# The remainder of the weights of tiles 2 to 15 computed on GpSimd, in a kernel whose list of instructions is made by a planner

## The chip, the core and the metric

The kernel runs on one core of a Trainium2 chip. The core has four engines that compute: TensorE (PE in the profile; its weight loads are PEld), VectorE (DVE), ScalarE (ACT) and GpSimd (POOL). SyncE (SP) starts the DMA transfers. Each engine works through its own queue in order, and the engines wait for each other by semaphores. The metric is the device time of one execution in microseconds; several runs are made, and their median counts.

## What is computed

Two stages follow one another: a linear recurrence over the sequence for each head, and a two-layer network on its output.

```python
for t in range(S):                                   # S = 768
    cur = einsum('bhd,bhe->bhde', u * k[t], v[t])
    y[t] = einsum('bhd,bhde->bhe', r[t], state + cur)
    state = w[..., None] * state + einsum('bhd,bhe->bhde', k[t], v[t])
x = y as (3072 tokens, 384)                          # 4 sequences, 8 heads of 48
h = x @ w_in                                         # 384 -> 2048
g = maximum(h, 0) + alpha * minimum(h, 0)
out = g @ w_out                                      # 2048 -> 384
```

All inputs and the output are 32-bit floats.

## The kernel before

**Tiles and stages.** The sequence is cut into 6 chunks of 128 tokens (`C`, `L`). For a chunk, the recurrence becomes a few matrix products for each of 4 pairs of heads (`attention(c, q, at)`), with the state carried from chunk to chunk. The network then works on the 512 tokens of a chunk (4 sequences of 128), in 16 tiles of 128 hidden units. A *step* is one tile of one chunk: `m_in(n)` makes the hidden units (three products for each of 3 blocks of rows, line 571) and applies the slope (lines 577 to 582); `m_out(n)` multiplies by the second matrix and adds up in `acc` (line 602), two to three steps later.

**Rounded part and rest.** A product of full precision is made of three products of a faster format: each operand is split into its rounded part and the rest. `xh` and `xl` are those of the activations, `gh` and `gl` those of the hidden units, `wh` and `wl` those of the weights. `wl` is the weight minus `wh`.

**The weights.** They come as words of eight bytes (64-bit floats), 768 KB for a tile. `weights(i, need)` turns tile i into 32-bit floats and splits it, once for all chunks: ScalarE makes a scaled magnitude (line 307), VectorE shifts it (309) and puts in the low bits and the sign (311, 314), ScalarE rounds to `wh` (317), VectorE subtracts to `wl` (318). The two halves of a tile's results stay in the memory on the core; the loaded words (`wraw`) and the 32-bit form (`wx`) have two buffers each. A `wx` buffer is free for the tile after next once line 318 has read it, a `wraw` buffer once line 314 has.

**Steps in order.** Chunks 0 and 1 take turns: tiles 0 to 8 of chunk 0, tiles 0 to 8 of chunk 1, tiles 9 to 15 of chunk 0, tiles 9 to 15 of chunk 1. So tile i of the first nine is needed at step i, and tiles 9 to 15 at steps 18 to 24. Then come chunks 2 to 5, 16 steps each.

**The planner.** The kernel doesn't issue instructions as it describes them. `add(engine, us, function, reads, writes, rank)` records a piece with an assumed duration. `Plan.in_order` runs a list schedule forward over all pieces (each engine takes the most urgent piece that is ready), then backward to get new urgencies, 12 times, keeps the round with the earliest end and sorts the pieces by their planned start. That list is the program: each engine's order is fixed by it, and the chip follows it however long things really take. Assumed durations on VectorE and ScalarE are shortened by a small overlap (0.08 and 0.1 us) when the engine is set free; GpSimd's are not. The planner holds nothing of one engine slowing another.

**Fillers.** Where the planner sees TensorE idle before the first piece of the network, it puts in small matmuls on the identity (`warm`, line 662 in the profile), which compute nothing that is used.

**GpSimd's own work.** Some tables at the start (lines 229 to 258 and 641); and for chunks 2 to 5 two products for each pair of heads (lines 394 and 396), which VectorE sums (line 400) into `cu`. ScalarE spreads `cu` over `base` (427), VectorE puts the scores over it (435), and TensorE uses `base` (479). For chunk 2, the piece of line 394 also names `wh` of tile 12 as something that it reads, so that in the list it stands behind it; on the chip it doesn't read it.

Of the kernel before, what the change touches and what calls it, by code (L numbers as in the profile page):

```python
# [56 lines left out]
class Plan:  # L57
# [12 lines left out]
    def add(self, eng, us, fn, r=(), w=(), rank=0.0, kb=0.0):  # L70
        p = Piece(eng, us, fn, r, w, rank, kb)
        for ref, wr in p.uses:
            b, part = ref if isinstance(ref, tuple) else (ref, None)
            log = self.log.setdefault(b, [])
            for other, opart, owr in log:
                if other is not p and (wr or owr) and (part is None or opart is None or part == opart):
                    p.after.add(other)
            log.append((p, part, wr))
        self.pieces.append(p)
        return p  # L80
# [92 lines left out]
def rwkv_prelu_kernel(ctx: ExitStack, tc, rk, vkr, wP, uP, u, wall, alpha, w, r_all, k_all, v_all, oT):  # L173
    nc = tc.nc
# [10 lines left out]
    add = plan.add  # L185

    def sb(shape, name, bufs, dt=F32):
        return plan.buf(lambda: wk.tile(shape, dt, name=name, bufs=bufs), name, bufs)
# [98 lines left out]
    def raw_weights(i, rank, behind=()):  # L287
        t = raws[i] = sb([128, 2 * DM, 2], "wraw", 2, U32)
        load(t, lambda: nc.sync.dma_start(t().rearrange("p f a -> p (f a)"), wall[i].bitcast(U32)), 768, rank, behind)
        return t  # L290

    def weights(i, need):


        raw = raws.get(i) or raw_weights(i, need - 9)
        h, l, t = wh[i], wl[i], sb([128, 2 * DM], "wx", 2, U32)

        def bits():
            return t()

        def x():
            return t().bitcast(F32)

        def hx():
            return h().rearrange("p k f -> p (k f)")

        add("ACT", 0.92, lambda: nc.scalar.activation(x(), raw()[:, :, 1].bitcast(F32), AF.Abs, scale=2.0 ** -112),
            r=[raw], w=[t], rank=need - 3 - 60 * (i == 0))
        add("DVE", 0.56, lambda: nc.vector.tensor_scalar(bits(), bits(), 3, None, op0=ALU.logical_shift_left), w=[t],
            rank=need - 2 - 60 * (i == 0))  # L310
        add("DVE", 0.95, lambda: nc.vector.scalar_tensor_tensor(
            out=bits(), in0=raw()[:, :, 0], scalar=29, in1=bits(), op0=ALU.logical_shift_right, op1=ALU.bitwise_or),
            r=[raw], w=[t], rank=need - 2 - 60 * (i == 0))
        add("DVE", 0.95, lambda: nc.vector.scalar_tensor_tensor(
            out=bits(), in0=raw()[:, :, 1], scalar=0x80000000, in1=bits(), op0=ALU.bitwise_and, op1=ALU.bitwise_or),
            r=[raw], w=[t], rank=need - 2 - 60 * (i == 0))
        add("ACT", 0.85, lambda: nc.scalar.activation(hx(), x(), AF.Copy), r=[t], w=[h], rank=need - 3 - 60 * (i == 0))
        add("DVE", 0.95, lambda: nc.vector.tensor_tensor(
            out=l().rearrange("p k f -> p (k f)"), in0=x(), in1=hx(), op=ALU.subtract), r=[t, h], w=[l], rank=need - 2 - 60 * (i == 0))


# [356 lines left out]
    for i in range(NF):  # L678
        jobs.append((need[i] - 8, 1, lambda i=i: weights(i, need[i])))
# [160 lines left out]
```

## Time and profile before

| | |
|---|---|
| median of 3 runs | 517.65 us (517.52 to 518.13) |
| the profiled run | 516.91 us |
| its span in the trace | 515.2 us |
| VectorE's line 318 | 16 instructions, 15.3 us in sum |
| GpSimd's lines 394 and 396 | 16 instructions each, 20.4 and 19.2 us in sum |

The span runs from the first to the last instruction that the profiler records; the time of the run is a little longer. A row such as `43.13 0.95 DVE L318 TENSOR_TENSOR wl<-wx,wh 128x768 ...` in the view in order of time says: at 43.13 us, for 0.95 us, VectorE ran the instruction of line 318, which wrote `wl` and read `wx` and `wh`; what stands in brackets behind it is how long the engine had been idle and who ended that. Small instructions on VectorE overlap a little, so that the start of the next one is the better measure of what one costs. In the view by source, three numbers with strokes are the shortest, median and longest duration in ns, followed by the first and the last start.

### The profile page before, as it was taken

To read this page: it belongs to the slowest core of one execution; us is meant where nothing else is said; L and a number is where in the kernel's file an instruction comes from. 1 tells how busy PE (TensorE), PEld (TensorE's weight loads), DVE (VectorE), ACT (ScalarE), POOL (GpSimd) and SP (SyncE) were. 2 spreads that over 40 slices of the span, in tenths; PEclk is the share of its full clock that TensorE was granted. 3 is DMA by queue.
4 is the path that set the end of the run, shared out by engine and by line. 5 is a ranking of instruction groups with operands and counts; after the bars stand their busy time and mean duration, and the time that the engine had idled before them with its cause. 6 is when DMAs were issued, how large, how long until landed. Compare 5 with 4: busy or idle time off the path is not lost.

```text
span 515.2 us, 9052 instructions
## 1 busy us (share of the span) xinstructions
PE 504.3 (98%) x3544; PEld 400.8 (78%) x3544; DVE 328.2 (64%) x577; ACT 242.8 (47%) x525; POOL 46.9 (9%) x54
## 2 busy tenths in 40 slices
PE   8999999999999999999999999999999999999994
PEld 6777887888877877787787777787777778888883
DVE  5899999999567885955674655674554453333331
ACT  2757665767455452543352652542643332322222
POOL 3020022010011020120110112030000000000000
PEclk9799999999999999999999999999999999999998
DMA  8864676551323721422120322120220000100001
GB/s 235 259 214 158 218 235 195 185 168 46 117 69 90 224 87 45 143 68 86 53 65 19 125 67 84 49 82 0 70 76 4 0 2 1 61 1 1 0 1 66
DMA packets 24880, 47.26 MB, mean 92 GB/s; under 512 B 4096, under 2 KB 12416, under 8 KB 24832
## 3 DMA queue, kind: packets, MB, share of 16 engines
q1 hardware_dynamic: 24832, 46.62, 28.7%
q8 instruction: 30, 0.49, 0.4%
q14 instruction: 18, 0.15, 0.1%
HBM read 37.96 MB, written 6.29 MB: 86 GB/s over the span
## 4 chain that ended last, share of the span: by engine, by line
PE 93%; DVE 3%; ACT 1%; DMA 1%; issue 1%; SPq 0%; DVEq 0%; ACTq 0%
PE acc L602 39%; PE hp L571 39%; PE A L411 3%; PE y L479 2%; PE y L474 2%; PE A L479 1%; PE A L420 1%; PE y L463 1%; PE y L488 1%; PE y L468 1%; ACT base L427 1%; DMA wp<-wP 1%; PE acc L384 1%; DVE raw L369 1%; PE acc L662 1%
## 5 line engine op out<-in xcount | busy, mean ns | idle before, releaser
L578 DVE SCALAR_TENSOR_TENSOR g<-hp,alph,g 128x512 f32<-128x512 f32 x96 | 71.9, 749 | 113.3 <-ACT g L577 113.1
L577 ACT ACTIVATE g<-hp 128x512 f32<-128x512 f32 x96 | 57.3, 597 | 145.8 <-PE hp L571 145.5
L571 PE MATMUL hp<-xh,wh 128*128 128x512 f32 x288 | 115.7, 402 | 0.8 <-DMA xh<-xh 0.8
L571 PE MATMUL hp<-xl,wh 128*128 128x512 f32 x288 | 113.8, 395 | 0.0
L571 PE MATMUL hp<-xh,wl 128*128 128x512 f32 x288 | 113.7, 395 | 0.0
L582 DVE TENSOR_TENSOR gl<-g,gh 128x512 fp32r<-128x512 f32 x96 | 68.6, 714 | 41.5 <-ACT gh L581 41.3
L581 ACT ACTIVATE gh<-g 128x512 fp32r<-128x512 f32 x96 | 60.6, 631 | 70.8 <-DVE g L578 70.5
L602 PE MATMUL acc<-gh,wh 128*128 128x512 f32 x288 | 85.2, 402 | 0.2 <-ACT gh L581 0.2
L602 PE MATMUL acc<-gh,wl 128*128 128x512 f32 x288 | 83.3, 396 | 0.0
L602 PE MATMUL acc<-gl,wh 128*128 128x512 f32 x288 | 82.7, 394 | 0.0
L571 PEld LDWEIGHTS hp<-xh,wh 128*128 128x128 f32 x288 | 54.0, 188 | 14.4 <-DMA xl<-xl 0.9
L602 PEld LDWEIGHTS acc<-gl,wh 128*128 128x128 f32 x288 | 54.0, 188 | 12.8
L602 PEld LDWEIGHTS acc<-gh,wl 128*128 128x128 f32 x288 | 53.8, 188 | 13.0
L571 PEld LDWEIGHTS hp<-xl,wh 128*128 128x128 f32 x288 | 54.1, 188 | 12.7
L571 PEld LDWEIGHTS hp<-xh,wl 128*128 128x128 f32 x288 | 54.1, 188 | 12.0
L602 PEld LDWEIGHTS acc<-gh,wh 128*128 128x128 f32 x288 | 52.4, 188 | 13.3 <-ACT gh L581 0.7
L427 ACT ACTIVATE base<-ident,cu 128x128 f32<-128x128 f32 x192 | 59.9, 390 | 1.0 <-DVE cu L400 0.7
L394 POOL TENSOR_TENSOR rr<-rr,kk 128x384 f32<-128x384 f32 x16 | 20.4, 1273 | 275.0 <-DMA kk<-vkr 136.5
L369 DVE TENSOR_TENSOR raw<-raw,W 112x512 f32<-112x512 f32 x45 | 36.7, 832 | 0.0
L435 DVE COPY_PREDICATED base<-strict,A 64x128 f32<-64x128 uint8 (+1 forms) x96 | 26.9, 343 | 0.8
L524 DVE TENSOR_TENSOR xl<-y,xh 48x256 fp32r<-48x256 f32 (+1 forms) x38 | 17.5, 462 | 3.0 <-ACT xh L523 2.6
L396 POOL TENSOR_TENSOR rr<-rr,utab 128x384 f32<-128x384 f32 x16 | 19.2, 1202 | 1.3
(102 smaller groups left out, 436.0 us busy)
## 6 DMA issues: line engine op xcount, KB each, us to landing
wraw<-wall SPq DMA_DIRECT2D x16, 768.0 KB, 4.9
raw<-rk SPq DMA_DIRECT2D x45, 224.0 KB, 2.9
v<-vkr SPq DMA_DIRECT2D x24, 192.0 KB, 3.6
kk<-vkr SPq DMA_DIRECT2D x24, 192.0 KB, 3.2
rr<-vkr SPq DMA_DIRECT2D x16, 192.0 KB, 2.5
oT<-o SPq DMA_DIRECT2D x12, 256.0 KB, 2.2
oT<-g SPq DMA_DIRECT2D x6, 256.0 KB, 2.7
xh<-xh SPq DMA_DIRECT2D x36, 32.0 KB, 2.2
```

Of the source, the lines that this page charges most:

```text
L369: add("DVE", 0.72, lambda t=t, tab=tab: nc.vector.tensor_tensor(out=t(), in0=t(), in1=tab().broadcast_to([112, B, L]), op=ALU.mult), r=[W[ ...
L394: add("POOL", 1.2, lambda: nc.gpsimd.tensor_tensor(out=rt(), in0=rt(), in1=k(), op=ALU.mult), r=[k] + ([wh[12]] if c == 2 else []), w=[rt] ...
L396: add("POOL", 1.2, lambda: nc.gpsimd.tensor_tensor(out=rt().rearrange("p (g b) e -> p g b e", g=2), in0=rt().rearrange("p (g b) e -> p g b ...
L427: add("ACT", 0.39, lambda g=g, b=b: nc.scalar.activation(base[g]()[:, b].rearrange("p (a t) -> p a t", a=2), ident().rearrange("p (a t) -> ...
L435: add("DVE", 0.42 if at_part is parts[0] else 0.28, lambda g=g, x=at_part: nc.vector.copy_predicated(base[g]()[x], strict4()[x], A[g]()[x] ...
L524: add("DVE", us + 0.1, lambda: nc.vector.tensor_tensor(out=view(l), in0=psum(), in1=view(h), op=ALU.subtract), r=[src] + refs(h), w=refs(l ...
L571: nc.tensor.matmul(hp(), a[i]()[:, k], x[c]()[:, k], start=(k == 0 and j == 0), stop=(k == NK - 1 and j == 2))
L577: add("ACT", 0.6, lambda: nc.scalar.activation(g(), hp(), AF.Copy), r=[hp], w=[g], rank=n - 100)
L578: add("DVE", 0.75, lambda: nc.vector.scalar_tensor_tensor(out=g(), in0=hp(), scalar=alph()[:, i:i + 1], in1=g(), op0=ALU.mult, op1=ALU.max ...
L581: add("ACT", 0.64, lambda: nc.scalar.activation(gh(), g(), AF.Copy), r=[g], w=[gh], rank=n - 100)
L582: add("DVE", 0.73, lambda: nc.vector.tensor_tensor(out=gl(), in0=g(), in1=gh(), op=ALU.subtract), r=[g, gh], w=[gl], rank=n - 99)
L602: nc.tensor.matmul(banks[k](), a[i]()[:, NK + k], x(), start=(begin and j == 0), stop=(end and j == 2))
```

## The change

```diff
@@ -315,7 +315,9 @@
         add("ACT", 0.85, lambda: nc.scalar.activation(hx(), x(), AF.Copy), r=[t], w=[h], rank=need - 3 - 60 * (i == 0))
-        add("DVE", 0.95, lambda: nc.vector.tensor_tensor(
+
+        on, eng, us = ("DVE", nc.vector, 0.95) if i < 2 else ("POOL", nc.gpsimd, 2.3)
+        add(on, us, lambda: eng.tensor_tensor(
             out=l().rearrange("p k f -> p (k f)"), in0=x(), in1=hx(), op=ALU.subtract), r=[t, h], w=[l], rank=need - 2 - 60 * (i == 0))
```

The subtraction at line 318 is recorded for GpSimd, with 2.3 us in place of 0.95, for tiles 2 to 15; tiles 0 and 1 keep VectorE. What it computes is the same. The planner then makes the whole list anew with the other engine and duration, so that the order of other pieces, and the fillers, can come out different too.

## The prediction

> **What bounds the kernel now.** I read the page first: the span, the busy shares and the shares of the chain that ended last. Then I cut the span into five stretches with the view of busy time by windows, whose columns are PE, PEld, DVE, ACT and POOL busy time (with instruction counts), the granted clock, the DMA share and GB/s.
>
> ```profile
> span 515.2 us, 9052 instructions
> PE 504.3 (98%) x3544; PEld 400.8 (78%) x3544; DVE 328.2 (64%) x577; ACT 242.8 (47%) x525; POOL 46.9 (9%) x54
> ...
> PE 93%; DVE 3%; ACT 1%; DMA 1%; issue 1%; SPq 0%; DVEq 0%; ACTq 0%
> ```
>
> ```profile
> 0.00:31.00 31.00, 27.78 (x247) 22.58 (x247) 22.48 (x46) 16.80 (x48) 5.69 (x22) 0.89 0.76 222
> 31.00:45.00 14.00, 12.91 (x121) 9.50 (x121) 13.92 (x22) 9.34 (x20) 1.64 (x1) 1.00 0.81 267
> 45.00:130.00 85.00, 85.00 (x582) 68.21 (x581) 83.67 (x130) 56.93 (x112) 7.89 (x6) 1.00 0.51 165
> 130.00:508.60 378.60, 378.59 (x2600) 300.48 (x2598) 208.16 (x383) 159.18 (x346) 31.67 (x26) 1.00 0.19 58
> 508.60:515.20 6.60, 0.00 (x0) 0.00 (x0) 0.00 (x0) 0.60 (x1) 0.00 (x0) 0.71 0.35 124
> ```
>
> The reader is to see two things in the windows. From 45.0 to 508.6 us TensorE has 0.01 us without work (85.00 of 85.00, then 378.59 of 378.60): its matmuls, not VectorE, set this length. And VectorE is full (83.67 of 85.00) just in 45 to 130, while TensorE is full beside it: a busy VectorE that TensorE does not wait for. What VectorE can give back lies only where TensorE still has gaps, in 31 to 45: 14.00 - 12.91 = 1.09 us. So the span is 31.0 + 14.0 + 463.6 + 6.6 = 515.2 us. The profiled run took 516.91 us, so 1.71 us lie around the span; the median of the three runs, 517.65, is 0.74 above that run.
>
> **What goes from VectorE.** The subtraction at line 318 is one group. Its row in the view by source (min/median/max ns, first and last start):
>
> ```profile
> L318 DVE TENSOR_TENSOR wl<-wx,wh x16: 946/952/1098, 27.2 to 128.7; 128x768 fp32r<-128x768 f32 x16
> ```
>
> Two of the 16 stay. Instructions overlap on VectorE: in the rows below L318 starts at 43.13 and the next one at 43.99, so one costs 0.86 us of the engine. 14 x 0.86 = 12.0 us leave VectorE, nearly all between 43 and 130 us, where TensorE has no gap. Worth to the span there: 0. No DMA goes with the step, and none is issued by it.
>
> ```profile
> 42.47 0.74 DVE L578 SCALAR_TENSOR_TENSOR g<-hp,alph,g 128x512 f32<-128x512 f32 x1
> 43.13 0.95 DVE L318 TENSOR_TENSOR wl<-wx,wh 128x768 fp32r<-128x768 f32 x1
> 43.99 1.02 DVE L499 TENSOR_TENSOR kk<-kk,wtok 128x384 f32<-128x384 f32 x2
> ...
> 41.98 0.84 ACT L317 ACTIVATE wh<-wx 128x768 fp32r<-128x768 f32 x1 [0.20 <-DVE wx L314]
> ...
> 43.93 0.96 PE L602 MATMUL acc<-gh,wh 128*128 128x512 f32 x3 [0.25 <-ACT gh L581]
> 44.96 0.39 PE L571 MATMUL hp<-xh,wl 128*128 128x512 f32 x1
> ```
>
> In 31 to 45 one single instance goes, tile 2's, at 43.13. The last gap of TensorE before 45 (0.25 us, ended at 43.93 by `gh`) hangs on the L578 at 42.47, which stands ahead of it. So the 0.86 us come too late to close a gap: 0 gained in this order.
>
> **What is added to GpSimd.** No row shows a 128x768 subtraction there. The nearest are its 128x384 products, half the size, and a tiny one:
>
> ```profile
> L394 POOL TENSOR_TENSOR rr<-rr,kk x16: 1010/1021/2445, 70.4 to 346.1; 128x384 f32<-128x384 f32 x16
> L396 POOL TENSOR_TENSOR rr<-rr,utab x16: 1002/1274/1519, 72.1 to 347.1; 128x384 f32<-128x384 f32 x16
> L258 POOL TENSOR_TENSOR uw<-up,wp x2: 284/431/578, 7.1 to 7.5; 48x4 f32<-48x4 f32 x2
> ```
>
> Lower end: 0.43 us of fixed cost (L258) plus 764/380 of (1.01 - 0.43) gives 1.6 us. Upper end: twice the 1.65 us that L394 took in the full stretch (rows below), 3.3 us. Twice the undisturbed 1.02 is 2.04, and I take 2.1, nearest to the medians. 14 x 2.1 = 29 us of GpSimd time from 43 us on; it worked 7.89 of 85 us there, so there is room.
>
> For tile 2: `wh` is done at 41.98 + 0.84 = 42.82, the result then at 44.9 (1.6: 44.4; 3.3: 46.1), and its first reader ran at 44.96. Between nothing and 1.2 us of a TensorE stall, once; the list knows a duration of 2.3, and TensorE has matmuls of tiles 0 and 1 left to put in front. I take 0.2. Nothing gets below zero by this term, as a later `wl` speeds nothing up.
>
> For tile 8, the last with little time in hand, the rows are:
>
> ```profile
> 86.49 0.96 DVE L318 TENSOR_TENSOR wl<-wx,wh 128x768 fp32r<-128x768 f32 x1
> ...
> 88.99 0.39 PE L571 MATMUL hp<-xh,wl 128*128 128x512 f32 x1
> ```
>
> 1.5 us between result and reader. GpSimd's extra 1.1 us fits; 3.3 us would be 0.8 late. Tiles 9 to 15 are read from step 18 on, which the chain in order of time has at 128.00, with 4.2 us from step to step:
>
> ```profile
> 96.52 1.82 DVE L318 TENSOR_TENSOR wl<-wx,wh 128x768 fp32r<-128x768 f32 x2
> ...
> 128.00 2.09 PE hp L571 x9
> ...
> 132.19 2.09 PE hp L571 x9
> ```
>
> Tile 9 is made at 97.5 and read at 128; tile 15, the last, is made at 129.7 and read six steps later, at 153: covered by more than 20 us.
>
> **The added wait.** L318 on GpSimd waits for ScalarE's L317. Behind it stand L394 and L396 of the third chunk, and VectorE's L400 waits for these. Before, GpSimd ran the first two pairs at 70 and 77 us, far ahead of L400; in the list L394 of that chunk stands behind `wh` of tile 12, so now subtractions are in front of it. Cover:
>
> ```profile
> 111.37 0.55 DVE L400 TENSOR_REDUCE cu<-rr 128x8 f32<-128x384 f32 x1
> 111.83 0.68 DVE L582 TENSOR_TENSOR gl<-g,gh 128x512 fp32r<-128x512 f32 x1
> ...
> 118.77 0.85 PE L602 MATMUL acc<-gl,wh 128*128 128x512 f32 x3
> 145.27 0.31 PE L479 MATMUL y<-base,v 128*48 128x128 f32 x1
> ```
>
> TensorE reads what comes of `cu` at 145.27, 33 us later, and the `gl` queued behind L400 at 118.77, 6.3 us after it is done. A late pair of 2 to 3 us costs nothing; without that cover it would cost its 2 to 3 us.
>
> **What GpSimd does to VectorE.** This is the term that the list does not hold. The three pairs in the full stretch, with VectorE beside them:
>
> ```profile
> 70.40 1.65 POOL L394 TENSOR_TENSOR rr<-rr,kk 128x384 f32<-128x384 f32 x1 [37.76 <-DMA kk<-vkr]
> ...
> 77.56 1.65 POOL L394 TENSOR_TENSOR rr<-rr,kk 128x384 f32<-128x384 f32 x1 [4.42 <-DMA kk<-vkr]
> ...
> 114.40 1.02 POOL L394 TENSOR_TENSOR rr<-rr,kk 128x384 f32<-128x384 f32 x1 [33.78 <-DMA rr<-vkr]
> 115.50 1.22 POOL L396 TENSOR_TENSOR rr<-rr,utab 128x384 f32<-128x384 f32 x1
> ...
> 78.88 0.87 DVE L369 TENSOR_TENSOR raw<-raw,W 112x512 f32<-112x512 f32 x1
> 80.34 1.10 DVE L318 TENSOR_TENSOR wl<-wx,wh 128x768 fp32r<-128x768 f32 x1
> 114.81 1.03 DVE L309 TENSOR_SCALAR wx<-wx 128x768 uint32<-128x768 uint32 x1
> 116.10 1.43 DVE L311 SCALAR_TENSOR_TENSOR wx<-wraw,wx 128x768 uint32<-128x768 uint32 x1
> ```
>
> ```profile
> L309 DVE TENSOR_SCALAR wx<-wx x16: 537/552/1026, 21.2 to 122.7; 128x768 uint32<-128x768 uint32 x16
> L311 DVE SCALAR_TENSOR_TENSOR wx<-wraw,wx x16: 943/950/1430, 22.9 to 125.2; 128x768 uint32<-128x768 uint32 x16
> L369 DVE TENSOR_TENSOR raw<-raw,W x45: 669/684/1502, 7.3 to 386.5; 112x512 f32<-112x512 f32 x45
> ```
>
> Against the medians the second pair cost VectorE 0.19 + 0.15 = 0.34 us and the third 0.48 + 0.48 = 0.96; beside the first nothing on VectorE was long. A pair moves as much data as one subtraction, so I take the mean, 0.43 us for each tile, with 0 and 0.96 as what pairs showed, and 2.04 (VectorE held for two whole products) as the far end. Net for VectorE: -0.86 + 0.43, with ends -0.86 and +1.18 us a tile. By the middle value the six tiles 3 to 8 leave VectorE 2.6 us ahead by 88 us, and it waits for TensorE: 0.
>
> The Trainium skill, page "SBUF — State Buffer", section "Who interferes with whom", says that GpSimd and VectorE share a port pair as an exclusive lock, and that the one that comes second is fully blocked. The 1.43 against 0.95 us at 116.10 agree in kind; that every GpSimd instruction blocks VectorE for its length the three pairs do not show, and what it would make of the sum is the first rival.
>
> **Sum.** 0 (to 31) + 0.2 (31 to 45) + 0 (45 to 508.6, fed TensorE) + 0 (the end: no instruction of it changes) = 515.4 us of span, 517.1 us for the run, and 517.65 + 0.2 = 517.85, given as **517.9 us**, as a median. About 0.2%, 1.0 us, is what a measurement of this kernel can tell from no change.
>
> **The rivals.**
>
> *VectorE blocked for nearly the whole subtraction* (slower). If VectorE loses c us per tile, it falls behind the old order by c - 0.86 a tile. Six tiles and 1.5 us in hand at tile 8: it costs 6 x (c - 0.86) - 1.5, from c = 1.11 us on. At c = 1.6, halfway from there to 2.04, that is 2.9 us: 520.6; at 2.04 it is 5.6 us, 523.3. For it: one instruction of 2 us leaves VectorE no turn in its middle, as a pair does, and most VectorE work of the weights (L309, L311) is of the kind that was held. Against it: c was 0.96 at most in three pairs. Chance 0.24.
>
> *A late `wl`* (slower or unseen). If a subtraction takes 3.3 us against the 2.3 in the list, TensorE waits 1.0 us at the first tile whose reader stands right behind; later tiles share this wait, since TensorE is then late already: 518.9. For: both early L394 took 1.65. Against: ScalarE had tile 2's `wh` done 0.31 us before VectorE took it up, and GpSimd is free sooner. Chance 0.10, half of it beyond 1.0 us.
>
> *A shorter start* (faster). The list is made anew, with 0.86 us less on VectorE before 45. If it puts tile 2's other steps and what follows forward, the 1.09 us of gaps go, and part of the filler matmuls of the start with them:
>
> ```profile
> 27.16 2.67 PE L662 MATMUL acc<-ident 128*128 128x256 bf16 x23
> 34.37 0.47 PE L571 MATMUL hp<-xh,wh 128*128 128x512 f32 x1 [0.76 <-DMA xh<-xh]
> ```
>
> 1.09 + 0.5 of the 2.67 gives 516.1. For: VectorE is full (13.92 of 14.00). Against: the larger gap, 0.76 us, ended with a DMA, and the fillers lie before any step that changes. Chance 0.24.
>
> **How the numbers follow.** The forecast, within 1.0 us of before, gets 0.42, with its own range 516.7 to 518.6; the rivals 0.24, 0.10 and 0.24. Faster by over 0.2%: 0.24, the shorter start. Slower: 0.24 and half of 0.10, 0.29. Within: 0.42 and the other half, 0.47. The range reaches to the shorter start's 516.1 and a little below, and to the blocked VectorE's 520.6: 515.7 to 520.6; outside lie a still shorter start (0.08) and c beyond 1.6 (0.10).
>
> **What would show it.** L318 should stand 14 times on POOL at 1.6 to 3.3 us, twice on DVE; TensorE's busy time in 45 to the end should be its length, and 31 to 45 hold about 1 us of gaps. VectorE's L309, L311 and L369 should be longer in sum by 14 x 0.43 = 6 us; 14 us or more would make the first rival, with TensorE's gaps between 50 and 90 us ended by VectorE's `xl`, `wx` or `raw`. Gaps ended by POOL `wl` L318 would make the second; a filler group shorter than 23 and no gap in 31 to 45 the third. The forecast is wrong if TensorE shows more than 1 us of new gaps behind 45, or works less before it.

## The result and the profile after

The changed kernel takes 529.44 us (median of 4 runs, 528.24 to 530.86) against 517.59 us before: a ratio of 1.0231, 95% interval 1.0205 to 1.0257, or 11.8 us more. The forecast was 517.9, with a range up to 520.6.

First the page of the changed kernel: its span, the busy shares, and the shares of the chain.

```profile
span 528.7 us, 9029 instructions
PE 509.4 (96%) x3536; PEld 402.9 (76%) x3536; DVE 333.8 (63%) x563; ACT 241.4 (46%) x525; POOL 71.5 (14%) x68
...
PE 81%; DVE 12%; issue 3%; DMA 1%; ACT 1%; SPq 0%; DVEq 0%; ACTq 0%
```

14 subtractions have left VectorE, some 12 us, and it is busy 5.6 us longer than before (333.8 against 328.2). Its share of the chain went from 3% to 12%. TensorE stands still for 528.7 - 509.4 = 19.3 us in place of 10.9, and works 5.1 us longer for the same products and fewer fillers; one reason is that half of its clock was granted for 10.2 us at the start and for 3.4 us at 131 us, in the kernel before for 6.8 us at the start alone (the end left out). Where it stands still, the busy time by windows tells (columns as in the prediction):

```profile
31.00:45.00 14.00, 11.79 (x118) 8.50 (x114) 13.92 (x22) 8.08 (x14) 1.67 (x2) 1.00 0.65 211
45.00:90.00 45.00, 41.79 (x328) 32.17 (x327) 43.20 (x55) 27.06 (x62) 14.70 (x7) 1.00 0.58 193
90.00:130.00 40.00, 36.80 (x220) 28.59 (x218) 36.26 (x42) 22.23 (x39) 16.07 (x10) 1.00 0.43 146
130.00:200.00 70.00, 69.82 (x521) 55.40 (x523) 48.59 (x90) 34.34 (x80) 11.51 (x9) 0.98 0.32 102
200.00:300.00 100.00, 100.00 (x776) 79.24 (x771) 64.81 (x123) 44.12 (x103) 11.48 (x10) 1.00 0.24 71
```

The gaps are in 31 to 130 us: 2.21 + 3.21 + 3.20 = 8.6 us, where there was 1.1. From 200 us on TensorE is full as before. The 6.4 us behind 45 us lie where GpSimd does the subtractions. The gaps before 45 us stand ahead of its first one (at 44.15 us) and have another cause (experiment 3).

The subtraction itself, in the view by source, and rows of VectorE that grew, in the groups by line and shape (busy us in sum, mean ns of one; the means before were 832, 979, 560 and 581):

```profile
L320 POOL TENSOR_TENSOR wl<-wx,wh x14: 1817/1846/3932, 44.1 to 139.1; 128x768 fp32r<-128x768 f32 x14
L320 DVE TENSOR_TENSOR wl<-wx,wh x2: 953/956/959, 27.7 to 37.6; 128x768 fp32r<-128x768 f32 x2
```

```profile
L371 DVE TENSOR_TENSOR raw<-raw,W 112x512 f32<-112x512 f32 x45 | 38.9, 887 | 1.6 <-DMA raw<-rk 1.5
L311 DVE SCALAR_TENSOR_TENSOR wx<-wraw,wx 128x768 uint32<-128x768 uint32 x16 | 24.2, 1510 | 0.2
...
L501 DVE TENSOR_TENSOR kk<-kk,wtok 128x384 f32<-128x384 f32 x20 | 13.5, 680 | 0.0
...
L309 DVE TENSOR_SCALAR wx<-wx 128x768 uint32<-128x768 uint32 x16 | 12.0, 748 | 2.7 <-ACT wx L307 2.7
```

(Lines from 318 on have moved by two: the subtraction is now line 320, and lines 307 to 317 are as they were.) One subtraction takes 1.85 us on GpSimd in the median: not the trouble. Line 311, one of the steps that stayed, has a mean of 1510 ns, where it had 979. Why shows in the order of time, GpSimd's and VectorE's rows at two places:

```profile
81.74 1.83 POOL L320 TENSOR_TENSOR wl<-wx,wh 128x768 fp32r<-128x768 f32 x1 [6.87 <-ACT wh L317]
...
96.71 1.83 POOL L320 TENSOR_TENSOR wl<-wx,wh 128x768 fp32r<-128x768 f32 x1 [7.93 <-ACT wh L317]
...
82.09 2.30 DVE L311 SCALAR_TENSOR_TENSOR wx<-wraw,wx 128x768 uint32<-128x768 uint32 x1
...
96.86 2.50 DVE L311 SCALAR_TENSOR_TENSOR wx<-wraw,wx 128x768 uint32<-128x768 uint32 x1
```

GpSimd began at 96.71 and ended at 98.54. VectorE's L311 began at 96.86 and ended at 99.36, that is 0.82 us, about its own length, after GpSimd's end: it made next to no progress until the subtraction was over. So did the one at 82.09. Each subtraction starts when ScalarE has `wh`. Beside 11 of the 14, one VectorE instruction was held like this: in seven cases the next tile's 309 (one operand) or 311 (two operands), in the others `kk`, `raw` or `gl`, all of which read from the memory on the core. These 11 took 14.4 us longer than the usual length of their kind. Three subtractions held nobody. The Trainium skill, "SBUF — State Buffer", section "Who interferes with whom", states that VectorE and GpSimd share a port pair as an exclusive lock. That the one that comes second is fully blocked it says of VectorE's two-port modes; here line 311, which reads two operands, shows the same.

It goes the other way too. GpSimd's first subtraction came while VectorE was busy, whose instructions kept their usual lengths, and took twice its usual time:

```profile
44.15 3.93 POOL L320 TENSOR_TENSOR wl<-wx,wh 128x768 fp32r<-128x768 f32 x1 [12.33 <-ACT wh L317]
...
43.70 1.02 DVE L501 TENSOR_TENSOR kk<-kk,wtok 128x384 f32<-128x384 f32 x2
44.64 0.68 DVE L371 TENSOR_TENSOR raw<-raw,W 112x512 f32<-112x512 f32 x1
45.24 0.68 DVE L584 TENSOR_TENSOR gl<-g,gh 128x512 fp32r<-128x512 f32 x1
```

Last, who held TensorE up, in the view of waits (in total, times, longest), and two windows around the longest:

```profile
PE hp L573 <- DVE g L580: 3.4, 2, 2.6
PE acc L386 <- DVE g L379: 1.7, 2, 0.9
PE acc L664 <- POOL ident L233: 1.5, 1, 1.5
PE y L490 <- DVE kk L501: 1.4, 1, 1.4
PE y L465 <- DVE base L440: 0.9, 2, 0.8
PE hp L573 <- POOL wl L320: 0.8, 1, 0.8
```

```profile
125.00:130.00 5.00, 2.58 (x11) 1.58 (x9) 5.00 (x6) 2.76 (x7) 1.74 (x2) 1.00 0.11 38
130.00:135.00 5.00, 4.82 (x14) 3.85 (x15) 4.88 (x11) 3.50 (x10) 3.27 (x2) 0.66 0.15 39
```

TensorE waited for a late `wl` once, 0.8 us (tile 2's, the slow one above). The longest wait is for line 580: the slope of the hidden units, which reads an `hp` bank and so frees it. It has nothing to do with weights; it stands behind them in VectorE's queue:

```profile
126.27 1.19 POOL L396 TENSOR_TENSOR rr<-rr,kk 128x384 f32<-128x384 f32 x1 [0.72 <-DMA rr<-vkr]
...
126.49 1.77 DVE L311 SCALAR_TENSOR_TENSOR wx<-wraw,wx 128x768 uint32<-128x768 uint32 x1
128.19 0.43 DVE L437 COPY_PREDICATED base<-strict,A 128x256 f32<-128x256 uint8 x1
128.52 0.94 DVE L314 SCALAR_TENSOR_TENSOR wx<-wraw,wx 128x768 uint32<-128x768 uint32 x1
129.39 0.74 DVE L580 SCALAR_TENSOR_TENSOR g<-hp,alph,g 128x512 f32<-128x512 f32 x1
```

The last hold before it, of L311 at 126.49, comes from a product of the recurrence on GpSimd (L396) and not from a subtraction; the subtractions had made VectorE late by then. After that gap of 2.6 us TensorE's granted clock is 0.66 in the next 5 us, so the gap is paid again in part.

### The profile page after: what moved, and what is told of

The parts are those of the page before. It is cut to its first block, busy times and chain, and to the rows that moved or that the text cites. A ratio compares the mean times of both kernels' runs of the same rounds, so it can differ in the third digit from the quotient of the medians.

```text
span 528.7 us, 9029 instructions
## 1 busy us (share of the span) xinstructions
PE 509.4 (96%) x3536; PEld 402.9 (76%) x3536; DVE 333.8 (63%) x563; ACT 241.4 (46%) x525; POOL 71.5 (14%) x68
## 4 chain that ended last, share of the span: by engine, by line
PE 81%; DVE 12%; issue 3%; DMA 1%; ACT 1%; SPq 0%; DVEq 0%; ACTq 0%
PE acc L604 35%; PE hp L573 34%; DVE wx L311 3%; PE A L413 3%; DVE wx L314 2%; PE y L481 2%; PE y L476 2%; PE A L481 1%; DVE g L580 1%; DVE raw L371 1%; DVE wx L309 1%; DMA raw<-rk 1%; DVE base L440 1%; PE y L490 1%; DVE kk L501 1%
## 5 line engine op out<-in xcount | busy, mean ns | idle before, releaser
L604 PEld LDWEIGHTS acc<-gh,wh 128*128 128x128 f32 x288 | 53.2, 189 | 13.4 <-ACT gh L583 0.5
L396 POOL TENSOR_TENSOR rr<-rr,kk 128x384 f32<-128x384 f32 x16 | 17.4, 1087 | 189.3 <-DMA kk<-vkr 135.6
L371 DVE TENSOR_TENSOR raw<-raw,W 112x512 f32<-112x512 f32 x45 | 38.9, 887 | 1.6 <-DMA raw<-rk 1.5
L320 POOL TENSOR_TENSOR wl<-wx,wh 128x768 fp32r<-128x768 f32 x14 | 28.5, 2036 | 71.6 <-ACT wh L317 58.6
L311 DVE SCALAR_TENSOR_TENSOR wx<-wraw,wx 128x768 uint32<-128x768 uint32 x16 | 24.2, 1510 | 0.2
```

Source lines behind the costliest of these rows:

```text
L311: add("DVE", 0.95, lambda: nc.vector.scalar_tensor_tensor(out=bits(), in0=raw()[:, :, 0], scalar=29, in1=bits(), op0=ALU.logical_shift_rig ...
L320: add(on, us, lambda: eng.tensor_tensor(out=l().rearrange("p k f -> p (k f)"), in0=x(), in1=hx(), op=ALU.subtract), r=[t, h], w=[l], rank= ...
L371: add("DVE", 0.72, lambda t=t, tab=tab: nc.vector.tensor_tensor(out=t(), in0=t(), in1=tab().broadcast_to([112, B, L]), op=ALU.mult), r=[W[ ...
L396: add("POOL", 1.2, lambda: nc.gpsimd.tensor_tensor(out=rt(), in0=rt(), in1=k(), op=ALU.mult), r=[k] + ([wh[12]] if c == 2 else []), w=[rt] ...
L604: nc.tensor.matmul(banks[k](), a[i]()[:, NK + k], x(), start=(begin and j == 0), stop=(end and j == 2))
```

## The experiments

The theories. **Held**: GpSimd's reads hold VectorE, and the time that VectorE loses, which the list doesn't know of, makes TensorE wait. **Order**: the loss belongs to the new list; in fact the planner kept another round's list. Its forecasts of the end, as the program computes them:

```text
before:  round 1: 509.21   rounds 2 to 12: 507.50
changed: round 1: 507.25   rounds 2 to 12: 507.55
```

The changed kernel takes the first round's list, which the planner put 0.30 us ahead of the others; before it was a second round's. **Late**: `wl` itself comes later. "Old list" below is the list of before, "new list" that of the changed kernel.

**1. The old list, GpSimd subtracting.**

```diff
-        add("DVE", 0.95, lambda: nc.vector.tensor_tensor(
+        add("DVE", 0.95, lambda: (nc.vector if i < 2 else nc.gpsimd).tensor_tensor(
```

> The list of before (planned for VectorE at 0.95 us), with the subtractions of tiles 2 to 15 issued to GpSimd in their places. Held theory (VectorE waits for whole subtractions): 4 to 9 us above before, the start as before (first hp at 31 us), and VectorE's two-input instructions long by 15 to 20 us in sum between 43 and 140 us. Order theory (the loss is the other list's): within 1 us of before. Late theory (wl comes later): slower, with TensorE's gaps ended by wl of line 318.

520.45 us, ratio 1.0058 (1.0030 to 1.0086): 3 us above before. The order theory's 1 us is too little, the held theory's 4 to 9 too much: VectorE lost 11.3 us (its page against that of experiment 9), less than the 15 to 20 expected. TensorE waited for `wl` once, 0.8 us. The start was as before.

**2. The new list, VectorE subtracting.**

```diff
-        add(on, us, lambda: eng.tensor_tensor(
+        add(on, us, lambda: nc.vector.tensor_tensor(
```

> The changed kernel's list, with the subtractions issued to VectorE in their places, so that GpSimd holds nobody but VectorE has 0.86 us a tile that the list does not know. Held theory: the 2.2 us of the start stay, and of the other 10 us at most half: 520 to 525 us. Order theory: all of it stays, 528 to 531 us.

524.22 us, ratio 1.0141 (1.0096 to 1.0185). Within the held theory's range; with the same list, taking GpSimd out saves 5 us.

**3. The new list, nobody subtracting.**

```diff
+            if p.eng == "POOL" and p.start > 20:
+                while zero:
+                    nc.gpsimd.memset(zero.pop()().bitcast(F32), 0.0)
...
-            out=..., in0=x(), in1=hx(), op=ALU.subtract)
+            out=..., in0=x(), in1=hx(), op=ALU.subtract) if i < 2 else None
```

> The changed kernel's list without the subtraction of tiles 2 to 15: their wl is set to zero by GpSimd in its idle time before 29 us, so no engine has the work and nobody is held. Held theory: 519 to 520.5 us, the later start alone. Order theory: 527 to 531 us. Late theory: 519 to 520.5 us too.

520.83 us, ratio 1.0074 (1.0049 to 1.0099), just above the 519 to 520.5 of the held and late theories and far from the order theory's 527 to 531. The new list by itself costs about 3.8 us; the other 8 of the 11.8 go with the subtractions. Where the 3.8 us are, this run's waits of TensorE between 31 and 140 us and its windows tell in good part:

```profile
PE y L490 <- DVE kk L501: 1.7, 1, 1.7
PE hp L573 <- DVE g L580: 0.8, 1, 0.8
PE hp L573 <- DMA xh<-xh: 0.4, 1, 0.4
PE A L422 <- DVE T L560: 0.3, 1, 0.3
```

```profile
31.00:45.00 14.00, 11.89 (x97) 8.51 (x96) 13.31 (x22) 6.86 (x13) 0.00 (x0) 0.88 0.68 214
45.00:90.00 45.00, 44.69 (x385) 35.74 (x384) 41.33 (x62) 30.88 (x67) 5.03 (x4) 1.00 0.60 191
```

TensorE stands still for 3.2 us, where it was 1.0 before, most of it for `kk` at 36 us; and behind that gap half of its clock was granted for 3.4 us, which by estimate is 1.7 us of work more. The changed kernel has the wait for `kk` too (1.4 us), without a fall of the clock there.

**4. The new list, GpSimd writing but not reading.**

```diff
...
+            eng.tensor_tensor(out=f[:, 0:1], in0=x()[:, 0:1], in1=hx()[:, 0:1], op=ALU.subtract)
+            for _ in range(2):
+                eng.memset(f[:, 1:].bitcast(F32), 0.0)
```

> The changed kernel's list; in place of a subtraction GpSimd subtracts one column and then writes zeros over the rest of wl twice, so that it is busy for about as long (1.5 to 2 us) but reads next to nothing, and the rest of the weights is left out. If VectorE is held by GpSimd's reads (held theory): 519.5 to 521.5 us and VectorE's instructions at their normal length. If any GpSimd work holds it: 526 to 530 us with long instructions. Late theory: 526 to 530 us with normal ones.

521.78 us, ratio 1.0079 (1.0046 to 1.0112): just above the range for reads, far from the others, and not to be told from experiment 3. GpSimd's groups between 40 and 150 us in this run:

```profile
L327 POOL MEMSET wl<- 128x767 f32 x28 | 21.0, 750 | 0.8
L325 POOL TENSOR_TENSOR wl<-wx,wh 128x1 fp32r<-128x1 f32 x14 | 5.1, 365 | 67.5 <-ACT wh L317 64.0 <-ACT cu L398 3.5
```

26.1 us of work after the same wait for `wh`, against 28.5 of subtractions, and `wl` ready about 1.9 us after `wh` as there: it costs nothing that could be told. Neither a later `wl` nor a busy GpSimd makes the loss; what is left is that it reads two operands. VectorE's two-operand instructions kept their length beside the writes (line 311 took 0.95 to 0.96 us). (The page "SBUF — State Buffer" of the Trainium skill, section "Who interferes with whom", has this too: two-input instructions contend with a GpSimd instruction that reads, not with one that only writes.) But writes are not free of holds: line 309, with one operand, took 1.05 us in place of 0.55 the two times that it started during a write, at 52.06 and 117.64 us:

```profile
51.17 1.53 POOL L327 MEMSET wl<- 128x767 f32 x2
...
52.06 1.05 DVE L309 TENSOR_SCALAR wx<-wx 128x768 uint32<-128x768 uint32 x1
```

**5. The planner's second round, GpSimd subtracting.**

```diff
-            if best is None or end < best[0]:
+            if n and (best is None or end < best[0]):
```

> The changed kernel with the planner's first round left out of the choice: it then takes the second round's list, planned at 507.55 us instead of 507.25 (before's list is a second round's too, at 507.50). Unplanned-time theory (the loss is VectorE's holds, 1.4 us a tile, that the list does not hold): the start as before (first hp at 31 us), and still 6 to 10 us lost between 43 and 140 us: 524 to 528 us. Order theory (a first round's list is the bad one): 519 to 521.5 us, as with before's list.

529.33 us, ratio 1.0264 (1.0212 to 1.0316), as slow as the changed kernel and above both ranges, though it starts early: its first `hp` ran at 30.2 us, and from 144 us on its steps ran 9.7 us behind those of before. So the round that the planner kept is not the cause.

**6. Time for the holds in the list.**

```diff
+        if i > 1:
+            add("DVE", 1.4, lambda: None, r=[t, h], rank=need - 2)
```

> The changed kernel, with 1.4 us of VectorE put into the list for each of the 14 subtractions (no instruction is issued for it), after wh and at the subtraction's rank. The list takes a second round's, planned at 509.08 us, 1.6 above before. Unplanned-time theory: VectorE is held as long as before (15 to 20 us in sum), but TensorE's gaps between 45 and 140 us fall to 0 to 2 us: 518 to 521 us. Order theory: 518 to 521 us as well. If holding itself costs, listed or not: 525 us and more.

524.83 us (521.58 to 527.37), ratio 1.0166 (1.0133 to 1.0199): above the range of both theories, and close to the 525 us given for holds that cost whether listed or not. The profiled run had a span of 519.9 us, with gaps until 150 us, the largest again `hp` for VectorE's `g` (2.9 us in three waits). That run was the fastest of the four, so the others show more loss than its trace. The interval lies below the changed kernel's, so the time in the list helps in part. Why it does not help more was not followed: VectorE was still held beside 12 of the 14 subtractions, as no instruction keeps the listed time free on the chip.

**7. The subtraction in two halves.**

```diff
...
+            for s in (slice(0, 2 * DM),) if i < 2 else (slice(0, DM), slice(DM, 2 * DM)):
+                eng.tensor_tensor(out=f[:, s], in0=x()[:, s], in1=hx()[:, s], op=ALU.subtract)
```

> The changed kernel's list, each subtraction on GpSimd cut into two instructions of 128x384, so that VectorE can have a turn between them, as between the products that the prediction measured on. Held theory: VectorE is late by 8 to 13 us in sum between 43 and 140 us instead of 19, and the time is 522 to 526 us. If a pair holds as long as one instruction: 528 to 531 us.

527.54 us, ratio 1.0192 (1.0163 to 1.0220), just above the range. VectorE is busy 330.2 us in place of 333.8, so a break in the middle gives back 3.6 us of holds, and little of the time.

**8. Only tiles 9 to 15 on GpSimd.**

```diff
-        on, eng, us = ("DVE", nc.vector, 0.95) if i < 2 else ("POOL", nc.gpsimd, 2.3)
+        on, eng, us = ("DVE", nc.vector, 0.95) if i < 9 else ("POOL", nc.gpsimd, 2.3)
```

> Only tiles 9 to 15 on GpSimd (the list, made anew, is a second round's at 507.50 us as before's). Unplanned-time theory: some 7 x 1.4 = 10 us of holds, but between 90 and 140 us, where what VectorE makes is used later: 0 to 3 us above before, 517.5 to 521 us. If every hold reaches TensorE as in the first tiles: 522 to 524 us.

523.59 us, ratio 1.0127 (1.0094 to 1.0160): a miss. These tiles are made 20 us ahead of use, and yet it costs 6.6 us. The waits of TensorE in that run:

```profile
PE hp L573 <- DVE g L580: 2.9, 2, 2.4
PE A L422 <- DVE raw L371: 1.7, 1, 1.7
```

Nobody waits for `wl`. TensorE waits for what stands behind the held instructions in VectorE's queue: the same line 580. How much of the 6.6 us the list itself costs is not known, as no run left the subtractions out of this one; in the profiled run 1.2 us came at the start, ahead of them (first `hp` at 32.21 us).

**9. The old list, nobody subtracting** (edit as in 3, on the kernel before).

> The list of before without the subtraction of tiles 2 to 15 on any engine (their wl is set to zero by GpSimd before 29 us, the rest of the weights is left out): VectorE has 12 us less to do and nobody is held. If VectorE's relief is worth nothing, as the prediction had it: 516.8 to 518.4 us, no difference. If TensorE did wait for it: 514 to 516.5 us.

516.59 us, ratio 0.9992 (0.9970 to 1.0014): no difference, with 10.4 us less of VectorE (its page has DVE 317.8 us). TensorE did not wait for the subtraction before. From 45 to 90 us VectorE has 38.66 us of work here, against 41.33 in the new list without the subtraction (experiment 3):

```profile
45.00:90.00 45.00, 44.08 (x406) 35.11 (x405) 38.66 (x61) 28.05 (x61) 5.06 (x4) 1.00 0.62 201
```

**10. The new list, VectorE subtracting one and a half times.**

```diff
...
+            nc.vector.tensor_tensor(out=f, in0=x(), in1=hx(), op=ALU.subtract)
+            if i > 1:
+                nc.vector.tensor_tensor(out=f[:, 0:DM], in0=x()[:, 0:DM], in1=hx()[:, 0:DM], op=ALU.subtract)
```

> The changed kernel's list with the subtractions on VectorE, each followed by a second subtraction of its first 384 columns: 0.86 + 0.47 = 1.33 us of VectorE a tile that the list does not know, 18.6 us in sum, as much as GpSimd held it, but on VectorE itself. If the time that VectorE loses is all that counts: 526 to 531 us, as the changed kernel. If holding harms in another way too (a later wl, the places where it falls): 524.5 to 526 us.

527.78 us, ratio 1.0199 (1.0168 to 1.0230). This interval and the changed kernel's overlap: 1.33 us a tile of plain work on VectorE does most of what GpSimd does to it, with GpSimd left out.

Put together, with the busy time of VectorE from row 1 of each page, beyond the 316.6 us of experiment 3:

| new list, tiles 2 to 15 | VectorE busy, us | beyond 316.6 | ratio to before |
|---|---|---|---|
| nobody subtracts (3) | 316.6 | 0 | 1.0074 |
| GpSimd writes only (4) | 318.6 | 2.0 | 1.0079 |
| VectorE subtracts (2) | 328.8 | 12.2 | 1.0141 |
| GpSimd, in halves (7) | 330.2 | 13.6 | 1.0192 |
| GpSimd (the change) | 333.8 | 17.2 | 1.0231 |
| VectorE, one and a half (10) | 336.0 | 19.4 | 1.0199 |

From top to bottom the time rises with what VectorE does that the list doesn't hold, but for the last row. Whether GpSimd's holds cost more than as much plain work is not shown: the intervals of neighbouring rows overlap, and the busy times are of one run each. 17.2 / 14 = 1.23 us for a subtraction on GpSimd, where on VectorE it took 0.87. The 11 instructions that were held right beside a subtraction account for 14.4 of the 17.2 us, 1.03 us for each of the 14; the rest was not followed one by one.

**11. and 12. The start.** In the changed kernel the first `hp` ran at 33.16 us, before at 30.96, ahead of the first GpSimd subtraction. TensorE's rows in order of time and the windows of the changed kernel's start:

```profile
7.78 1.02 PE L386 MATMUL acc<-uw,g 112*128 112x2 f32 x8 [0.85 <-DVE g L379]
...
10.79 1.02 PE L386 MATMUL acc<-uw,g 112*128 112x2 f32 x8 [0.90 <-DVE g L379]
```

```profile
10.00:15.00 5.00, 4.21 (x30) 4.00 (x31) 5.00 (x15) 4.19 (x15) 0.00 (x0) 0.68 1.05 350
15.00:20.00 5.00, 5.00 (x41) 4.43 (x43) 2.07 (x6) 2.61 (x9) 0.00 (x0) 0.50 1.05 292
20.00:25.00 5.00, 5.00 (x51) 4.05 (x47) 5.00 (x9) 3.05 (x8) 0.00 (x0) 0.80 0.77 247
```

Half of its clock was granted from 12 to 22 us, in the kernel before from 13 to 20. But this differs between traces of one list. In those of the new list, half speed at the start lasted 6.8 us in experiments 3 and 10, with the first `hp` at 31.53 and 32.10, and 10.2 us in the changed kernel and experiments 2, 4 and 7, with the first `hp` at 32.87 to 33.44. So the late start of one trace is not the new list's alone. The kernel before varies in the same way: of 22 runs beside experiments 9 to 12, the one with the highest mean granted clock, 0.994, took 514.34 us, and the one with the lowest, 0.983, took 519.15.

Fillers were added, in the changed kernel (8 in each of two gaps) and in the one before (`{1: 8, 5: 5}` in place of `{1: 8, 3: 8}`):

```diff
+    pe = [p for p in order if p.eng == "PE"]
+    for n, more in {1: 8, 3: 8}.items():
+        fill[pe[n]] += more
```

> The changed kernel with 8 more filler matmuls in each of TensorE's gaps at 6.9 and 9.9 us. If its later start is TensorE's clock (half speed from 11.9 to 22 us instead of 13 to 19.6): the half speed is shorter or gone, the first hp at 30 to 32 us instead of 33.2, and 526.5 to 528.5 us. If the order alone makes the start: first hp at 33 us or later, 529 to 531 us.

> The kernel before with more filler matmuls in its gaps at 7.7 us (8) and 13.1 us (5), nothing else changed. If the clock costs it time at the start too: no or less half speed between 13 and 20 us, the first hp at 29.5 to 30.5 us, 516 to 517 us, below before. If transfers and VectorE set the start: first hp at 31 us, 517.5 to 518 us.

In the changed kernel the clock stayed full until 34 us and the first `hp` ran at 29.5 us, 3.6 us earlier; then TensorE stood for 3.9 us, and its clock fell to half behind that gap:

```profile
PE hp L573 <- DMA xh<-xh: 3.9, 1, 3.9
PE hp L573 <- DVE g L580: 3.4, 2, 2.6
```

The second step started at 38.07 in place of 38.44, and the time is 528.19 us (ratio 1.0194, 1.0156 to 1.0232), not to be told from 529.44. In these traces the clock accounts for the late first product, but the copies of `xh` bound what comes next. In the kernel before, the fillers did not close the gap (0.80 us for VectorE's `raw`), half speed came at 11.1 us and lasted to 21.4, the first `hp` ran at 32.8, and it took 518.65 us (ratio 1.0023, 1.0002 to 1.0044): if anything slower, and a miss for both expectations. No version here that computes everything beats the kernel before.

## Why the prediction was wrong

- *"0 (45 to 508.6, fed TensorE)"* is the step of the sum that failed. From 45 to 131 us TensorE stood still for 6.4 us, before for 0.01: 5.6 us of it for VectorE (lines 580, 440, 560 and 526), 0.8 for `wl`. By experiments 2 to 4, some 8 of the 11.8 us go with the subtractions on GpSimd and their reading, and 3.8 with the new list. What stood behind the zero is answered one by one.
- *"Worth to the span there: 0"*, for what leaves VectorE: right. Experiment 9 took it away without GpSimd and found a ratio of 0.9992.
- *The duration on GpSimd, 2.1 us between 1.6 and 3.3*: right in the median, 1.85 us; but tile 2's took 3.93, above the range, as VectorE was at its own instructions first. Its late `wl`, taken at 0.2 us, cost 0.8.
- *"A pair moves as much data as one subtraction, so I take the mean, 0.43 us for each tile"*: this term was too small. It measured 1.23 us a tile by VectorE's busy time, and 1.03 by the held instructions alone: above the 0.96 taken for the worst pair and above the 0.87 that the change frees. Three pairs were too few, and two of them show the other direction. VectorE's L314 began at 70.23 and at 77.38, each time 0.2 us before GpSimd's L394, and it was L394 that then took 1.65 us in place of 1.02. The prediction read these 1.65 us as a duration and the pairs as mild. The halves of experiment 7 cost 13.6 / 14 = 0.97 us a tile, more than twice the pairs'. Nor do the subtractions fall at random: ScalarE's `wh` releases them, and in half of the cases VectorE was then just at the next tile's 309 or 311. The two rows of VectorE before:

```profile
70.23 0.94 DVE L314 SCALAR_TENSOR_TENSOR wx<-wraw,wx 128x768 uint32<-128x768 uint32 x1
...
77.38 0.94 DVE L314 SCALAR_TENSOR_TENSOR wx<-wraw,wx 128x768 uint32<-128x768 uint32 x1
```

- *The sign given for the first rival*, lines 309, 311 and 369 longer by 14 us in sum: it came close, with 2.7 + 8.5 + 2.2 = 13.4 us.
- *"Net for VectorE: -0.86 + 0.43"*, and the first rival's price of 6 x (c - 0.86) - 1.5: the rival's mechanism was right, its sum wrong. A c of 1.23 gives 0.7 us by it, and one of 1.03 nothing; the subtractions cost 8. The 0.86 us was counted as time in hand, and in the new list it is not: there 12.2 us of plain subtractions put back on VectorE cost 3.4 us (experiments 2 and 3), in the old list 10.4 us cost nothing that could be told (experiment 9). The planner had filled part of the freed time with other work (41.33 against 38.66 us from 45 to 90). Even in the old list, which keeps the 0.86 free, 329.1 - 317.8 = 11.3 us of holds cost 3 us (pages of experiments 1 and 9).
- *"Tiles 9 to 15 ... covered by more than 20 us"*: true of `wl`, and beside the point. The cover was measured to the reader of `wl`; what had to be measured was the cover of everything that stands behind the held instructions in VectorE's queue. Experiment 8 put only these tiles on GpSimd and lost 6.6 us, its own list included.
- *The late pair behind L400*: no wait of TensorE names it, as said. But its products hold VectorE too, and one did so just ahead of TensorE's longest wait (L311 at 126.49).
- *The re-made list* was taken at 0, or as a gain of 1.6 us. It cost about 3.8 us (experiment 3). That experiment 5, with another list of the same pieces, is as slow, says that the loss is not peculiar to the first round. In the trace of experiment 3, 2.2 us of new waits, above all for `kk`, and about 1.7 us from half the clock add up to it. This is one trace; why the planner's order brings `kk` late stays open.

## What to carry to other kernels

Before moving an elementwise step from VectorE to GpSimd, count it against VectorE: here 0.87 us of work became 1.0 to 1.2 us of standing still, and the engine that was to be relieved had more to do. Where a list or a schedule is made with assumed durations, time taken off an engine is no full reserve, as the schedule fills part of it; what it doesn't know of piles up in the in-order queue. And the cover of a late instruction is that of the tightest one queued behind it, not that of its own result.

## What the runs showed of the hardware

A GpSimd instruction that only writes left VectorE's two-operand instructions alone (28 writes of 128x767, 750 ns each; line 311 took 0.95 to 0.96 us beside them, experiment 4), but it held line 309, which reads one operand, from 0.55 to 1.05 us. One that reads two operands from the memory on the core held a VectorE instruction from 0.95 to 2.50 us. Where VectorE's two-operand instruction had begun first, GpSimd's took longer instead: 1.65 us in place of 1.02 (line 394 at 70.40 and 77.56 us in the kernel before), and 3.93 in place of 1.85 (line 320 at 44.15 us).

TensorE's granted clock fell to half soon after short gaps: in the changed kernel at 11.8 us, after 0.85 and 0.90 us of standing still before 7.8 and 10.8 us, for ten microseconds; with these gaps filled it stayed full until a gap of 3.9 us. Not each gap of this kind does it: 1.45 us of standing still before 37.88 us left the changed kernel's clock full, while 1.68 us at the same place in experiment 3 was followed by half speed. In all 14 traces the stretches of half speed, but for the one at the end, lasted 3.4, 6.8 or 10.2 us.
